# Late sums of a Strassen-like second product, and four weight sums, as accumulating DMAs from GpSimd's queue

## The chip, the cores and the metric

The kernel runs on one core of a Trainium2 chip. The metric is the device time of one execution in microseconds (us), the median of the runs shown. The engines are named as in the profile: PE is TensorE's matmul and PEld its weight load, DVE is VectorE, ACT is ScalarE, POOL is GpSimd, SP is SyncE, which here only issues DMAs.

## What is computed

The reference runs a gated linear recurrence over 768 steps for 4 batches and 8 heads of 48, joins the heads to rows of 384, and puts each row through a normalisation and a two-layer network with a residual. All of it is float32.

```python
for t in range(S):
    state = alpha[:, :, t, :, None] * state + np.einsum('bhd,bhe->bhde', k[:, :, t], v[:, :, t])
    y[:, :, t] = np.einsum('bhd,bhde->bhe', q[:, :, t], state)
x = y.transpose(0, 2, 1, 3).reshape(B, S, H * D)
xn = (x - mean(x)) / np.sqrt(var(x) + 1e-06) * g_ln
out = x + np.maximum(xn @ w_ch1, 0.0) @ w_ch2        # 384 -> 1536 -> 384
```

## The kernel before

The 768 steps are cut into six chunks of 128 (c = 0 to 5). For each chunk and batch a routine `attention` makes the rows x, stores them in DRAM (`kept`), normalises and transposes them to `xT`. Chunk 0 goes through the network in the plain way. Chunks 1 to 5 take both matrix products in a scheme with fewer block products than blocks: sums of blocks are formed first, then 15 block products (`hidden_product`) make the hidden layer and 20 (`product`) make the output, and each product is added to or subtracted from several output parts.

The order of everything is written out by hand. `ORDER` is a string of letters, each of which advances one generator by a step: `M` the products of chunks 1 to 4 and the second product of chunk 5, `V` the first product of chunk 5, `N` the sums of hidden blocks (`combine_hidden`), `X` the sums of x blocks (`combine_x`), `W` the sums of w2's blocks (`combine_weights`), lower-case letters `attention`, `A` and the other capitals up to `L` the weights. Each engine then executes its own instructions strictly in that order and waits on semaphores.

In `product(c, n)` the number n names one of 20 block products and comes in the order `SECOND`, which ends 6, 12, 5, 9, 8, 4, 13, 17, 7, 16. Each is four float32 matmuls (line 618) that accumulate into one PSUM bank of 128x192; there are eight banks (`tag="bank"`), shared with all other matmuls. VectorE takes the product out of PSUM and adds it (`add`, line 628) or subtracts it (`sub`, line 631). The targets are `o(0)` to `o(7)`, the halves of the four output tiles `ob`, which were loaded with x, and five scratch parts `e`, `f`, `g`, `q4`, `r8` in three tiles `u`. A `late` sum (line 634) adds one such part to another on GpSimd:

- n = 6: after VectorE's `sub(o(1))`: `late(o(1), e)`, `late(o(1), f)`, then `send(c, 0)`;
- n = 5: VectorE makes g, then `late(f, g)`;
- n = 9: VectorE's `sub(f)`, then `late(o(2), f)`, `late(o(3), f)`, then `send(c, 1)`;
- n = 13: VectorE's `add(q4)`, then `late(o(5), q4)`, `late(o(5), g, "sub")`, `late(r8, q4, "sub")`, `late(o(7), r8)`, `late(o(6), r8)`;
- n = 7 and n = 16: VectorE's `add(o(5))` and `add(o(6))`, each followed by a send.

These are ten late sums in a chunk, eight additions and two subtractions. `send` (line 497) issues a store on SP's queue, where loads for `attention` stand too (line 122 and 172 alpha, k and q; line 493 reloads `ob`; lines 316 and 378 move gate rows). On GpSimd's queue stand also the gate products of `attention` (line 403) and the late sums of the hidden products (lines 814 to 834).

`combine_weights` (line 578) makes 13 sums of 128x768 of w2's six blocks b[0] to b[5] on VectorE, some into tiles of their own (t8, n6, n2, n5 and others), some in place (b[3], b[5]). The framework tracks the tiles: an instruction that overwrites a tile waits for those that still read it.

Of the kernel before, what the change touches and what calls it, by code (L numbers as in the profile page):

```python
# [14 lines left out]
AOP = mybir.AluOpType  # L15
# [34 lines left out]
def kernel(  # L50
# [36 lines left out]
    nc = tc.nc  # L87
# [5 lines left out]
    NCB = S // P  # L93
# [402 lines left out]
    def send(c, b, cols=slice(0, DM)):  # L496
        nc.sync.dma_start(out[b, c * P:(c + 1) * P, cols], ob_of[c, b][:, cols])
# [54 lines left out]
    def weights_ready():  # L552

        if "b" not in win:
            b = {(t, h): w2[:, t * NT:(t + 1) * NT, h * HM:(h + 1) * HM]
                 for t in range(3) for h in range(2)}
            win["b"] = {4: b[2, 0], 7: b[0, 1], 11: b[2, 0], 14: b[1, 0], 15: b[1, 0], 17: b[0, 0]}
        return win["b"]

    def combine_weights():  # L560
        spare = [stage.tile([P, NF, 2 * P], INT64, name="ws", tag="ws") for _ in range(3)]
        spare = [t.rearrange("p a c -> p (a c)").bitcast(FP32) for t in spare]
        new = [t[:, i * NT * HM:][:, :NT * HM].rearrange("p (j m) -> p j m", m=HM)
               for t in spare for i in range(2)] + [
            more[:, i].rearrange("p (j m) -> p j m", m=HM) for i in range(4)]
        b = [w2[:, t * NT:(t + 1) * NT, h * HM:(h + 1) * HM] for t in range(3) for h in range(2)]
        t8, t9, t12, t1, n0, n6, n2, n13, n5, n10 = new
        add, sub = nc.vector.tensor_add, nc.vector.tensor_sub
        ready = weights_ready()
        for ns, op, o, x, y in (  # L570
                ((8,), add, t8, b[1], b[5]), ((12, 18), sub, t12, b[4], b[5]),
                ((1, 19), sub, t1, b[2], b[3]), ((9,), sub, t9, b[1], b[3]),
                ((6,), add, n6, t9, b[5]), ((), add, b[3], b[0], b[4]),
                ((3,), sub, b[5], b[3], b[2]), ((16,), sub, b[3], b[3], t8),
                ((2,), add, n2, t9, b[4]), ((5,), add, n5, t9, b[2]),
                ((10,), sub, n10, b[0], n5), ((0,), sub, n0, t8, b[2]),
                ((13,), sub, n13, t8, b[4])):
            op(o, x, y)
            ready |= {n: o for n in ns}
            yield  # L580

    def blocks_of(c):
        if c not in win:
            win[c] = a = [third_of(c, t, b // HB)[:, :, b % HB] for b in range(B) for t in range(3)]
            win["a", c] = {1: a[10], 3: a[0], 4: a[8], 10: a[3], 14: a[7], 16: a[9], 17: a[6],
                           18: a[5]}
        return win[c], win["a", c]
# [23 lines left out]
    def product(c, n):  # L611
        if n == SECOND[0]:
            u = [work.tile([P, 512], FP32, name="u", tag="sum", bufs=11) for i in range(3)]
            win["u"] = [u[i // 2][:, i % 2 * HM:][:, :HM] for i in range(5)]
        acc = ps.tile([P, HM], FP32, name="ops", tag="bank", bufs=8)
        lhs, rhs = blocks_of(c)[1][n], weights_ready()[n]
        for j in range(NT):
            nc.tensor.matmul(acc, lhs[:, j], rhs[:, j], start=(j == 0), stop=(j == NT - 1))  # L618
        yield
        e, f, g, q4, r8 = win["u"]  # L620

        def o(k):
            return ob_of[c, k // 2][:, k % 2 * HM:][:, :HM]

        copy = nc.scalar.copy

        def add(x):
            nc.vector.tensor_add(x, acc, x)  # L628

        def sub(x):  # L630
            nc.vector.tensor_sub(x, x, acc)  # L631

        def late(x, y, op="add"):
            getattr(nc.gpsimd, f"tensor_{op}")(x, x, y)  # L634

        if n == 15:
            copy(out=e, in_=acc)
            add(o(0))
        elif n == 3:
            add(o(0))  # L640
        elif n == 11:
            copy(out=f, in_=acc)
            sub(o(0))
        elif n == 2:
            nc.vector.tensor_sub(f, acc, f)
        elif n == 18:
            sub(o(1))
            sub(o(3))
        elif n == 10:
            add(o(2))  # L650
        elif n == 19:
            sub(o(3))
            add(o(5))
        elif n == 0:
            add(e)
        elif n == 1:
            sub(o(1))
            sub(o(7))
        elif n == 6:
            sub(o(1))  # L660
            late(o(1), e)
            late(o(1), f)
            send(c, 0)
        elif n == 14:
            copy(out=g, in_=acc)
            add(o(4))
        elif n == 5:
            nc.vector.tensor_sub(g, acc, g)
            late(f, g)
        elif n == 9:  # L670
            sub(f)
            late(o(2), f)
            late(o(3), f)
            send(c, 1)
        elif n == 8:
            nc.vector.tensor_add(r8, acc, e)
        elif n == 4:
            copy(out=q4, in_=acc)
            add(o(4))
        elif n == 17:  # L680
            add(o(4))
        elif n == 12:
            sub(o(5))
            add(o(7))
        elif n == 13:
            add(q4)
            late(o(5), q4)
            late(o(5), g, "sub")
            late(r8, q4, "sub")
            late(o(7), r8)  # L690
            late(o(6), r8)
        elif n == 7:
            add(o(5))
            send(c, 2)
            send(c, 3, slice(HM, DM))
        else:
            add(o(6))
            send(c, 3, slice(0, HM))
        yield
# [165 lines left out]
    def second_of_chunk_0(h):  # L865
        for i in range(3):
            for b in range(2 * h, 2 * h + 2):
# [4 lines left out]
    turns |= {chr(ord("a") + n): attention(n // B, n % B) for n in range(NCB * B)}  # L872
    turns |= {chr(ord("A") + i): take_weights(i) for i in range(len(pieces))}
    turns |= {"M": mlp(), "V": hidden_products(NCB - 1), "S": combine_first(), "W": combine_weights(), "R": relus(),
              "X": (x for c in range(1, NCB) for x in combine_x(c)),
              "N": (x for c in range(1, NCB) for x in combine_hidden(c)), "O": outputs()}
# [32 lines left out]
```

## Time and profile before

| | |
|---|---|
| median of 3 runs | 434.89 us (433.16 to 435.3) |
| span of the profiled execution | 431.0 us |
| its own whole time | not given apart; the median lies 3.9 us above the span |
| PE busy | 425.7 us, 99% of the span |
| DVE, ACT, POOL busy | 333.2, 200.0, 152.7 us |
| mean granted TensorE clock | 0.999 |
| line 634, additions and subtractions into `ob` | 40, 27.0 us busy, mean 685 ns |
| line 634, into `u` | 10, 6.9 us busy, mean 691 ns |
| line 578 | 13 sums, 0.95 us each |

A row of the timeline gives the start, the duration, the engine, the line, the operation, its output and inputs, how many were merged, and in brackets how long the engine had been idle and who ended that. "POOL ob L634 <- DVE ob L631" in the waits means that GpSimd's instruction of line 634 waited for VectorE's of line 631. The idle time of an engine that is not on the chain to the end costs nothing.

### The profile page before, as it was taken

How to read it: one execution, taken by the hardware profiler on the slowest of the kernel's cores; microseconds unless marked ns; L12 is line 12 of the kernel's file. 1: busy time of each engine (PE TensorE's matmuls, PEld its weight loads, DVE VectorE, ACT ScalarE, POOL GpSimd, SP SyncE). 2: the span in 40 equal slices, each digit the busy share in tenths (PEclk: the TensorE clock that was granted, in tenths of full speed). 3: DMA queues.
4: the chain of work that ended last, by engine and by line, in shares of the span. 5: the costliest groups of instructions: out<-in, count | busy, mean ns of one | idle time of the engine just before them, and what ended most of it. 6: DMA issues, size and time to landing. Idle time of an engine off the chain costs nothing.

```text
span 431.0 us, 11676 instructions
## 1 busy us (share of the span) xinstructions
PE 425.7 (99%) x4760; PEld 378.2 (88%) x4760; DVE 333.2 (77%) x644; ACT 200.0 (46%) x519; POOL 152.7 (35%) x164
## 2 busy tenths in 40 slices
PE   8999999999999999999999999999999999999997
PEld 6788888866588889998889998889998899999996
DVE  4989899999998888866769756757686668948683
ACT  6597466774043882325385134384415562221100
POOL 1011031110205382252563243580153661647423
PEclk9999999999999999999999999999999999999999
DMA  8979968774117354031150141400014000011201
GB/s 287 288 208 272 308 151 257 203 247 142 38 56 212 107 148 141 29 105 45 52 151 23 49 120 38 94 2 22 2 56 146 2 1 2 0 39 37 75 18 55
DMA packets 55517, 45.53 MB, mean 106 GB/s; under 512 B 26748, under 2 KB 51580, under 8 KB 55464
## 3 DMA queue, kind: packets, MB, share of 16 engines
q1 hardware_dynamic: 54920, 44.63, 35.0%
q8 instruction: 37, 0.61, 0.6%
q10 hardware_dynamic: 544, 0.17, 0.2%
q14 instruction: 16, 0.13, 0.1%
HBM read 35.25 MB, written 9.53 MB: 104 GB/s over the span
## 4 chain that ended last, share of the span: by engine, by line
PE 94%; DVE 2%; DMA 1%; ACT 1%; SPq 0%; issue 0%; DVEq 0%
PE hps L795 30%; PE ops L618 30%; PE ops L518 7%; PE hps L506 6%; PE tps L336 4%; PE aps L360 3%; PE ups L388 2%; PE yps L426 2%; PE yps L429 2%; PE xps L476 2%; DMA ws<-in_moe_w_ch_dram 1%; PE lps L303 1%; PE aps L352 1%; PE lps L244 1%; PE lps L298 1%; PE yps L414 1%
## 5 line engine op out<-in xcount | busy, mean ns | idle before, releaser
L795 PE MATMUL hps<-sum,w 128*128 128x256 f32 x192 | 48.0, 381 | 0.0
L634 POOL TENSOR_TENSOR ob<-ob,u 128x192 f32<-128x192 f32 x40 | 27.0, 685 | 58.9 <-DVE ob L631 44.3
L618 PE MATMUL ops<-w,hT 128*128 128x192 f32 x224 | 40.7, 328 | 0.0
L795 PEld LDWEIGHTS hps<-sum,w 128*128 128x128 f32 x192 | 35.7, 190 | 4.7 <-ACT hT L825 0.2
L618 PEld LDWEIGHTS ops<-w,hT 128*128 128x128 f32 x224 | 36.9, 190 | 1.0 <-issue 0.6
L403 POOL TENSOR_TENSOR mid<-mid,gate 112x192 f32<-112x192 f32 x20 | 13.3, 668 | 68.7 <-DVE mid L401 19.7
L795 PE MATMUL hps<-xT,w 128*128 128x256 f32 x136 | 34.4, 380 | 0.0
L506 PE MATMUL hps<-xT,w 128*128 128x256 f32 x144 | 34.0, 384 | 0.1
L846 ACT ACTIVATE hT<-hT 128x512 f32<-128x512 f32 x48 | 28.8, 625 | 10.4 <-POOL hT L817 7.1
L518 PE MATMUL ops<-w,hT 128*128 128x384 f32 x96 | 32.8, 490 | 0.0
L628 DVE TENSOR_TENSOR ob<-ops,ob 128x192 f32<-128x192 f32 x50 | 17.6, 353 | 17.7 <-PE ops L618 9.4
L506 PEld LDWEIGHTS hps<-xT,w 128*128 128x128 f32 x144 | 26.3, 190 | 4.0 <-DVE xT L479 0.6
L618 PE MATMUL ops<-ws,sum 128*128 128x192 f32 x160 | 29.2, 327 | 0.0
L814 POOL TENSOR_TENSOR hT<-hT,u 128x512 f32<-128x512 f32 x8 | 10.4, 1305 | 53.0 <-DVE u L813 53.0
L795 PEld LDWEIGHTS hps<-xT,w 128*128 128x128 f32 x136 | 25.5, 190 | 3.2
L518 PEld LDWEIGHTS ops<-w,hT 128*128 128x128 f32 x96 | 17.6, 190 | 10.5
L618 PEld LDWEIGHTS ops<-ws,sum 128*128 128x128 f32 x160 | 26.4, 190 | 0.2
L336 PE MATMUL tps<-consts,qk 128*112 128x128 f32 x176 | 25.3, 275 | 0.2 <-DVE qk L311 0.2
L336 PEld LDWEIGHTS tps<-consts,qk 128*112 128x112 f32 x176 | 20.3, 134 | 4.3 <-DVE qk L311 0.8
L460 ACT ACTIVATE xn<-x,few 128x384 f32<-128x384 f32 x24 | 14.8, 615 | 18.7 <-DVE few L456 17.5
L618 PE MATMUL ops<-ws,hT 128*128 128x192 f32 x128 | 23.4, 327 | 0.0
L618 PE MATMUL ops<-more,sum 128*128 128x192 f32 x120 | 22.0, 327 | 0.0
(243 smaller groups left out, 1172.9 us busy)
## 6 DMA issues: line engine op xcount, KB each, us to landing
ws<-in_moe_w_ch_dram SPq DMA_DIRECT2D x12, 768.0 KB
vn<-in_v_dram SPq DMA_DIRECT2D x12, 384.0 KB
kept<-x SPq DMA_DIRECT2D x24, 192.0 KB
ob<-kept SPq DMA_DIRECT2D x24, 192.0 KB
out_dram<-ob SPq DMA_DIRECT2D x19, 192.0 KB
ra<-in_alpha_dram SPq DMA_DIRECT2D x14, 192.0 KB
rk<-in_k_dram SPq DMA_DIRECT2D x6, 384.0 KB
rq<-in_q_dram SPq DMA_DIRECT2D x6, 384.0 KB
```

The costliest lines, as they stand in the source:

```text
L336: nc.tensor.transpose(tps[:, p], qk_of(c, b)[:, i, p].rearrange("p a b -> p (a b)")[:, :R], ident)
L360: nc.tensor.matmul(aps[0][halves[i if cross else 1 - i], p, s], kT[rs, p, s], qT[rs, p, s], start=True, stop=True)
L403: nc.gpsimd.tensor_mul(new, new, by)
L460: act(out=xn, in_=x, func=AFT.Square, bias=mean, accum_out=dev)
L506: nc.tensor.matmul(hps, w1[:, j // 2, f, j % 2 * P:][:, :P], xT_of[0][:, f, bs], start=(f == 0), stop=(f == NF - 1))
L518: nc.tensor.matmul(ops_of[b], hT_of[c][:, j, b], w2[:, j], start=(j == 0), stop=(j == NJ - 1))
L618: nc.tensor.matmul(acc, lhs[:, j], rhs[:, j], start=(j == 0), stop=(j == NT - 1))
L628: nc.vector.tensor_add(x, acc, x)
L634: getattr(nc.gpsimd, f"tensor_{op}")(x, x, y)
L795: nc.tensor.matmul(acc[:, i], w, b, start=True, stop=True)
L814: add_late(c4, c4, u2)
L846: nc.scalar.activation(out=x, in_=x, func=AFT.Relu)
```

## The change

Two places change. In `combine_weights`, an addition whose target is not b[3] becomes a copy of the first operand by ScalarE and a DMA, issued from GpSimd's queue, that adds the second operand to it in the DMA's path. This holds for t8, n6, n2 and n5, of 128x768. In `product`, a `late` addition in chunks 1 to 4 becomes such a DMA of 128x192; late subtractions, and all late sums of chunk 5, stay GpSimd's elementwise instructions. That makes 4 DMAs of 384 KB and 32 of 96 KB, SBUF to SBUF. Each completes through a semaphore of its own kind, so an instruction that reads or overwrites what the DMA reads or writes, on any engine, the queue of GpSimd included, now waits for its landing.

```diff
@@ combine_weights
-            op(o, x, y)
+            if op is add and o is not b[3]:
+                nc.scalar.copy(out=o, in_=x)
+                nc.gpsimd.dma_start(o, y, accum_op=AOP.add)
+            else:
+                op(o, x, y)
@@ product
         def late(x, y, op="add"):
-            getattr(nc.gpsimd, f"tensor_{op}")(x, x, y)
+            if op == "add" and c + 1 < NCB:
+                nc.gpsimd.dma_start(x, y, accum_op=AOP.add)
+            else:
+                getattr(nc.gpsimd, f"tensor_{op}")(x, x, y)
```

The changed program's queues show the order: within a chunk GpSimd's second DMA into o1 waits for the first, the one into f for the second, VectorE's `sub(f)` for that one, GpSimd's subtraction from o5 for the DMA into o5, and the store of each half for the DMA that wrote it. VectorE's in-place difference into b[5] waits for the DMAs into t8 and n6, and n10 for the one into n5.

## The prediction

> **What bounds the kernel now.** I read the page first, then the chain of waits in the stretch of the four weight sums, then the timelines of chunk 1's late sums.
>
> ```profile
> PE 425.7 (99%) x4760; PEld 378.2 (88%) x4760; DVE 333.2 (77%) x644; ACT 200.0 (46%) x519; POOL 152.7 (35%) x164
> ...
> PE 94%; DVE 2%; DMA 1%; ACT 1%; SPq 0%; issue 0%; DVEq 0%
> ```
>
> TensorE is busy for 425.7 of 431.0 us and is 94% of the chain that ended last. GpSimd (POOL), which the change relieves, is busy 35% and is not on that chain. So work that is moved off POOL or VectorE saves at most the 5.3 us in which PE is idle, while any wait that reaches PE is paid in full.
>
> The chain asked for 108 to 162 us, where twelve of w2's thirteen sums run, has this header and holds nothing but PE:
>
> ```profile
> by line: PE hps L795 49.2%; PE ops L518 24.6%; PE yps L426 6.0%; PE aps L360 5.6%; PE tps L336 4.9%; PE ups L388 3.9%; PE yps L429 3.6%; PE lps L303 1.5%; PE xps L476 1.2%
> ```
>
> The timeline of chunk 1's late sums on POOL (start, duration, engine, line, op; in brackets the idle time before and who ended it):
>
> ```profile
> 179.85 1.64 POOL L634 TENSOR_TENSOR ob<-ob,u 128x192 f32<-128x192 f32 x2 [13.01 <-DVE ob L631]
> 182.96 0.77 POOL L634 TENSOR_TENSOR u<-u 128x192 f32<-128x192 f32 x1 [1.00 <-DVE u L668]
> 184.26 2.24 POOL L634 TENSOR_TENSOR ob<-ob,u 128x192 f32<-128x192 f32 x2 [0.53 <-DVE u L631]
> 188.97 1.37 POOL L634 TENSOR_TENSOR ob<-ob,u 128x192 f32<-128x192 f32 x2 [2.01 <-DVE u L628]
> 190.31 0.59 POOL L634 TENSOR_TENSOR u<-u 128x192 f32<-128x192 f32 x1
> 190.97 1.14 POOL L634 TENSOR_TENSOR ob<-ob,u 128x192 f32<-128x192 f32 x2
> ```
>
> In order: o1+=e, o1+=f; f+=g; o2+=f, o3+=f; o5+=q4, o5-=g; r8-=q4; o7+=r8, o6+=r8. The consumers, from the timelines of VectorE, PE, SP and ACT:
>
> ```profile
> 183.83 0.35 DVE L631 TENSOR_TENSOR u<-u,ops 128x192 f32<-128x192 f32 x1 [0.28 <-POOL u L634]
> 184.10 0.95 DVE L578 TENSOR_TENSOR more<-ws,w 128x768 f32<-128x768 f32 x1
> ...
> 195.26 0.36 DVE L628 TENSOR_TENSOR ob<-ops,ob 128x192 f32<-128x192 f32 x1 [0.69 <-PE ops L618]
> ```
> ```profile
> 187.04 1.46 PE L618 MATMUL ops<-more,sum 128*128 128x192 f32 x8
> ```
> ```profile
> 186.53 0.35 SPq L497 DMA_DIRECT2D out_dram<-ob  x1
> 186.94 2.07 SPq L122 DMA_DIRECT2D ra<-in_alpha_dram  x2
> ```
> ```profile
> 190.95 0.52 ACT L292 ACTIVATE la<-ra 128x384 f32<-128x384 f32 x1 [2.42 <-DMA ra<-in_alpha_dram]
> ```
>
> VectorE's subtraction at 183.83 already waits for POOL's f+=g; the n13 weights (184.10) come behind it, PE needs them 2.0 us after they are done (187.04), and alpha's loads stand in SP's queue behind a send that waits for o2 and o3.
>
> **The price of one accumulating DMA.** 32 replace POOL adds of 128x192 (0.69 us mean), eight in each of chunks 1 to 4; four replace 128x768 adds of w2. No row shows one. The nearest for 128x192: the ten sends of the same 96 KB from SP, which by the trace's semaphore records land 1.61 to 1.76 us (median 1.71) after their issue starts, 0.34 of it issuing. Below that I see no reason to go except for POOL's own 0.69, the price at which nothing changes. The far row above: alpha's 96 KB loads, at most 6.72. My value, an estimate: 1.71, plus 0.66 because I take 1.0 us of issue on POOL (between SP's 0.34 and the 1.3 that POOL takes for a 128x512 add), plus 0.29 for a second operand (eight 768 B packets to a DMA engine at 36 ns), plus 0.3 for traffic (`ob<-kept` lands in 2.16 quiet, 2.77 at the median): D = 3.0. For w2's 384 KB the nearest are the 384 KB loads of v, 3.31 to 7.44, and below them `ob<-kept` at 2.16 for half the bytes: Db = 4.2.
>
> The Trainium skill (DMA: Bandwidth & Descriptors, the SWDGE path) fits a DMA from this queue as 2.0 us plus bytes over 436 GB/s, end to end. By it, an estimate, D would be 2.2 and Db 2.9 for plain copies, and the sum below about 12 us instead of 23; no row here shows this queue.
>
> **w2's sums.** Removed: four VectorE adds of 0.95 us. The chain of that stretch is PE alone, so this gains nothing. Added: four ACT copies of 128x768, about 0.87 each (COPY 128x512 takes 0.58, ACTIVATE 128x768 1.02), and four DMAs. The first (n8) has ACT idle for 12.33 us around it: free. The second (n6) stands on ACT behind line 440 and starts at 127.1, so its DMA is issued at 128.0 and lands at 132.2; the VectorE subtraction b5, which overwrites a source of that DMA, started at 127.37 and becomes 4.9 us late. Behind it in VectorE's queue stands the L805 evacuation (129.16) on which PE's matmuls at 130.19 depend, 0.34 after its end: PE loses 4.6. The last two (n2, n5) are copied one behind the other from 144.8 and issued at 145.7 and 146.7; n5 lands at 150.9. The subtraction n10, begun at 147.06, is 3.8 late; PE's transposes of qk at 150.92 have 1.9 of cover: 1.9 lost.
>
> **Chunk 1.** o1's two DMAs write the same half row and the third writes f, which the second reads, so the three land one after the other: 3D from 179.85. The subtraction moves from 183.83 to 179.85 + 9.0: 5.0 late. Two gate products (L403, 181.45 and 186.47) stand on POOL behind these waits, and VectorE's state sum for the first; they move inside the same 5 us. PE's cover of 2.0 leaves 3.0. But o2 and o3 are then issued at 189.3 and 190.3 and land at 193.3, and SP sends at 193.3 instead of 186.53; the alpha loads behind it, the logarithm at 190.95 (already ended by that DMA) and PE's lps matmul at 191.52 all move by 6.8. This contains the 3.0. The tail of the chunk stays within it: o5's DMA, then POOL's two subtractions (0.7 each), o7's issue and o6's landing take D + 1.4 + 1.0 + D = 8.4 from 188.97 against a consumer at 195.26, 2.1 late on top of 3.0. **6.8.**
>
> **Chunk 2.** Late sums start at 242.02, the subtraction at 246.32: 9.0 - 4.3 = 4.7 late; PE's next need of a sum behind it (252.02, ready 248.84) covers 3.2: 1.5. Tail: 251.36 + 1.5 + 8.4 = 261.3 for the o6 add that stood at 255.24, 6.0 late; chunk 3's x sums stand behind it and PE's hidden products need them, with 0.8 of cover and 0.5 of VectorE idle: **4.7** in all.
>
> **Chunk 3.** 311.13 and 314.99: 5.1 late; the sum made at 315.27 is needed at 317.32, cover 1.4: 3.7. The tail's 7 us of lateness meets PE running ahead into free PSUM banks (eight hidden products of 0.865 us): about 0.7 left. **4.4.**
>
> **Chunk 4.** 379.47 and 385.64: 2.8 late, cover 3; its products alternate with hidden products of the last chunk: **0.8**.
>
> In chunks 2 and 3 ob's reloads and gate rows stand in SP's queue behind late sends too; their readers come a stage later, and I give that nothing.
>
> Sum: 4.6 + 1.9 + 6.8 + 4.7 + 4.4 + 0.8 = 23.2. The profiled execution spans 431.0, so about 454.2; the runs' median is 434.89, 3.9 above that span, which I leave as it is: **458 us**. Each us of D adds about 13 (4 + 5 + 3 + 1), each us of Db about 2.
>
> **Rivals.** *Hidden:* if a DMA cost no more than the add it replaces (D about 0.7), 3D is 2.1 against gaps of 3.9 to 6.2 and nothing in the chunks is late; w2's Db of 1 leaves 1 to 2 us. 435 to 437. For it: POOL is idle 65%. Against: no transfer in this trace lands so soon. Chance 0.05.
> *Not slower, rather faster:* VectorE's freed 3.8 us pull in its later instructions at 110 to 148 us. This needs n6 on time, that is a landing by 127.7, before its DMA can be issued (128.0) unless the ACT copy runs earlier; and the chain there has no VectorE. At most 3.8: 431. Chance 0.02.
> *Heavy DMA:* reading, adding and writing back near the longest landings, D of 4.6 to 6.7: 23 + 13 x 1.6 to 3.7, and w2's 3 to 5 more: 481 to 511. For it: loaded rows do reach 6.7. Against: traffic after 160 us is low. Chance 0.11.
> *Cold clock:* PE's waits become 3 to 6 us long where the longest idle now is 0.8. At the start PE took 3.78 us for 16 matmuls of 128 columns (0.236 each) where later four take 0.44 (0.11): half speed, lasting some 5.5 us, so a restart costs up to 2.7; four of them about 11: 469. Chance 0.10. The Trainium skill (TensorE: Matmul & The Clock Gate, Part 1) names such a rule: idle for a window of some 3.4 us halves the clock. The opening rows agree that PE begins at half speed; nothing here shows it going back in mid-kernel.
> *The forecast,* D of 1.7 to 4.6: chance 0.72. Its low end: D = 1.71 with issue 0.34 and Db = 2.8 leaves 2.8 for w2 and 1.0 for chunk 1, the rest covered: 439. Its high end 481.
>
> **Numbers.** 458 us. 439 to 497 leaves out the hidden and the faster case (0.07), of the heavy one what lies above 497 (0.06), and a little at the forecast's low end (0.05). About 0.5% (2.2 us) is what a measurement can tell from no change: slower 0.92, same 0.06, faster 0.02.
>
> **What would show it.** PE's busy time stays near 426 while its span grows; VectorE waits at the subtraction of f, at b5 and n10 and at the o6 add, ended by DMAs; the late-sum stretch of chunk 1 on POOL grows from 12 to about 20 us; ACT's wait for alpha at chunk 1 grows to 9. I am wrong if landings are under 1.7 or over 4.6, if PE's granted clock drops, or if PE's lost time sits elsewhere, such as at the end, where chunk 5 is unchanged.

## The result, and the profile after

The changed kernel takes 477.9 us (median of 4 runs, 473.48 to 478.84) against 434.65 for the one before: 1.097 times as long, 95% interval 1.092 to 1.103. That is 43 us more, where 23 were forecast. The profiled execution took 477.57 us and spans 475.8.

The page after. First the busy times; then, out of the 40 slices of the span, TensorE's busy tenths and its granted clock:

```profile
PE 441.0 (93%) x4760; PEld 387.8 (82%) x4760; DVE 327.3 (69%) x640; ACT 203.4 (43%) x523; POOL 162.7 (34%) x168
...
PE   7999999999959699969999977999969999999796
...
PEclk9999999999979999989999997999989999999899
```

The number of matmuls is the same, but two things grew. TensorE's idle time went from 5.3 us (431.0 less 425.7) to 34.8 (475.8 less 441.0): 29.5 us of waits. Its busy time went from 425.7 to 441.0: 15.3 us in which nothing was added. The second row explains this: slices with a clock digit of 7 or 8, where before every digit was 9. The trace's clock events show six stretches at half clock, 3.4 us long or twice that, 30.7 us in all. Each begins in a gap of TensorE's work or less than 1 us behind one. TensorE stood idle for 4.3 of these 30.7 us, so about half of the other 26.4 is lost; compared matmul by matmul with the kernel before, 13.8 of the 15.3 us lie inside the six stretches. The sum 29.5 + 15.3 = 44.8 is the growth of the span.

TensorE's rows at the longest gaps, from three stretches of its timeline (in brackets the idle time before and who ended it):

```profile
136.41 2.08 PE L802 MATMUL hps<-sum,w 128*128 128x256 f32 x4 [4.87 <-DVE hT L812]
...
163.63 0.65 PE L336 MATMUL tps<-consts,qk 128*112 128x128 f32 x4 [4.31 <-DVE qk L309]
...
287.88 1.65 PE L802 MATMUL hps<-sum,ra 128*128 128x256 f32 x3 [5.53 <-DVE sum L776]
```

VectorE is named as the one that ended them. The table of waits says what VectorE and POOL were themselves waiting for (sum in us, times, longest):

```profile
DVE u L635 <- DMA u<-u: 19.1, 4, 6.1
...
DVE ob L632 <- DMA ob<-u: 9.8, 3, 3.6
...
POOL ob L641 <- DMA ob<-u: 8.0, 4, 2.6
...
POOL ob L639 <- DMA ob<-u: 7.8, 4, 2.0
...
DVE more L582 <- DMA more<-w: 7.6, 1, 7.6
...
DVE w L582 <- DMA ws<-w: 6.9, 1, 6.9
```

None of these rows exists before. L635 is the subtraction from f, L632 an accumulation into ob, L641 POOL's two late subtractions, L639 the late DMAs themselves, L582 the sums of w2. The stretch of POOL that the prediction showed for chunk 1, in the kernel after:

```profile
194.74 0.89 POOL L639 DMA_DIRECT2D ob<-u  x1 [13.58 <-DVE ob L635]
197.53 0.86 POOL L639 DMA_DIRECT2D ob<-u  x1 [1.91 <-DMA ob<-u]
...
200.61 0.87 POOL L639 DMA_DIRECT2D u<-u  x1 [1.68 <-DMA ob<-u]
203.85 1.73 POOL L639 DMA_DIRECT2D ob<-u  x2 [2.38 <-DVE u L635]
...
208.12 0.88 POOL L639 DMA_DIRECT2D ob<-u  x1 [2.01 <-DVE u L632]
211.60 0.58 POOL L641 TENSOR_TENSOR ob<-ob,u 128x192 f32<-128x192 f32 x1 [2.59 <-DMA ob<-u]
212.15 0.58 POOL L641 TENSOR_TENSOR u<-u 128x192 f32<-128x192 f32 x1
213.03 1.74 POOL L639 DMA_DIRECT2D ob<-u  x2 [0.30 <-POOL u L641]
```

The stretch of 12 us before now lasts 20. POOL waits in its own queue for one DMA before it issues the next. The consumers are, on VectorE, TensorE, SP and ACT:

```profile
203.19 0.35 DVE L635 TENSOR_TENSOR u<-u,ops 128x192 f32<-128x192 f32 x1 [3.87 <-DMA u<-u]
203.46 0.95 DVE L582 TENSOR_TENSOR more<-ws,w 128x768 f32<-128x768 f32 x1
```
```profile
204.47 2.11 PE L622 MATMUL ops<-more,sum 128*128 128x192 f32 x8 [2.61 <-DVE more L582]
...
213.10 0.54 PE L303 MATMUL lps<-la,consts 64*64 64x384 f32 x2 [2.34 <-ACT la L292]
```
```profile
208.04 0.35 SPq L497 DMA_DIRECT2D out_dram<-ob  x1
208.44 1.13 SPq L122 DMA_DIRECT2D ra<-in_alpha_dram  x2
```
```profile
212.52 0.52 ACT L292 ACTIVATE la<-ra 128x384 f32<-128x384 f32 x1 [5.04 <-DMA ra<-in_alpha_dram]
```

The subtraction from f waits 3.87 us for the third landing; the w2 sum n13 (L582) stands behind it, and TensorE's product that needs n13 stalls 2.61. SP holds alpha's loads behind the send of o2 and o3, ACT's logarithm waits 5.04 for them, and TensorE stalls 2.34 more.

The view of the DMA issues gives the price of one (KB each, median us from issue to landing; single small ones took up to 4.3, the large ones 4.9 to 6.7):

```profile
ob<-u POOLq DMA_DIRECT2D x28, 96.0 KB, 2.6
...
ws<-w POOLq DMA_DIRECT2D x2, 384.0 KB, 5.1
more<-w POOLq DMA_DIRECT2D x2, 384.0 KB, 5.8
u<-u POOLq DMA_DIRECT2D x4, 96.0 KB, 2.8
```

The page counts 36 DMAs: 32 late sums (28 into ob, 4 into u) and four for w2. The expectations below miscount them: where they say 28 late transfers it is 32 (3.15 of the 4.72 MB), 36 in all, and 20 in the tail.

### The profile page after: what moved, and what is told of

Its sections match the earlier page's. It is cut to its first block, busy times and chain, and to the rows that moved or that the text cites. A ratio compares the mean times of both kernels' runs of the same rounds, so it can differ in the third digit from the quotient of the medians.

```text
span 475.8 us, 11724 instructions
## 1 busy us (share of the span) xinstructions
PE 441.0 (93%) x4760; PEld 387.8 (82%) x4760; DVE 327.3 (69%) x640; ACT 203.4 (43%) x523; POOL 162.7 (34%) x168
## 3 DMA queue, kind: packets, MB, share of 16 engines
q0 software_dynamic: 6720, 4.72, 7.4%
## 5 line engine op out<-in xcount | busy, mean ns | idle before, releaser
L802 PE MATMUL hps<-sum,w 128*128 128x256 f32 x192 | 50.7, 397 | 4.9 <-DVE hT L812 4.9
L802 PEld LDWEIGHTS hps<-sum,w 128*128 128x128 f32 x192 | 37.4, 200 | 10.4 <-DVE hT L812 5.3
L639 POOL DMA_DIRECT2D ob<-u x28 | 24.3, 955 | 59.1 <-DVE ob L635 32.8
L622 PE MATMUL ops<-w,hT 128*128 128x192 f32 x224 | 43.2, 342 | 0.8 <-DVE u L635 0.8
L632 DVE TENSOR_TENSOR ob<-ops,ob 128x192 f32<-128x192 f32 x50 | 17.6, 352 | 34.4 <-DMA ob<-u 9.8
L622 PEld LDWEIGHTS ops<-w,hT 128*128 128x128 f32 x224 | 39.3, 200 | 2.0 <-DVE u L635 1.1
L853 ACT ACTIVATE hT<-hT 128x512 f32<-128x512 f32 x48 | 29.0, 625 | 14.4 <-POOL hT L824 10.6
L460 ACT ACTIVATE xn<-x,few 128x384 f32<-128x384 f32 x24 | 14.8, 615 | 38.0 <-DVE few L456 36.9
L622 PE MATMUL ops<-more,sum 128*128 128x192 f32 x120 | 24.0, 347 | 6.2 <-DVE sum L609 3.6
L622 PEld LDWEIGHTS ops<-more,sum 128*128 128x128 f32 x120 | 21.3, 202 | 7.0 <-issue 3.9
L622 PEld LDWEIGHTS ops<-ws,sum 128*128 128x128 f32 x160 | 26.4, 190 | 0.2
L518 PEld LDWEIGHTS ops<-w,hT 128*128 128x128 f32 x96 | 17.5, 190 | 10.5
```

The source lines that it names most:

```text
L460: act(out=xn, in_=x, func=AFT.Square, bias=mean, accum_out=dev)
L518: nc.tensor.matmul(ops_of[b], hT_of[c][:, j, b], w2[:, j], start=(j == 0), stop=(j == NJ - 1))
L639: nc.gpsimd.dma_start(x, y, accum_op=AOP.add)
L802: nc.tensor.matmul(acc[:, i], w, b, start=True, stop=True)
L853: nc.scalar.activation(out=x, in_=x, func=AFT.Relu)
```

## The experiments

Theory W: landings are waited for inside the queues of VectorE, GpSimd and SyncE, gaps in TensorE follow, and its clock falls behind them. Against it stand: load as such (L), accumulation as what makes the DMA slow (A), a clock that falls for another reason or at no cost (C), and a price paid by each landing wherever it stands (E). Gains and losses below are against the runs of the kernel before that were made beside each group (434.5, 433.08 and 433.42 us for the first, second and third).

### The two parts apart

Late sums only: w2's sums stay on VectorE (the first hunk of the change is left out).

```diff
-            getattr(nc.gpsimd, f"tensor_{op}")(x, x, y)
+            if op == "add" and c + 1 < NCB:
+                nc.gpsimd.dma_start(x, y, accum_op=AOP.add)
+            else:
+                getattr(nc.gpsimd, f"tensor_{op}")(x, x, y)
```

> Only the late sums of the second product (28 transfers of 96 KB) are accumulating DMAs; w2's four sums stay on VectorE. Theory W (the loss is landings that VectorE, GpSimd and SyncE wait for in their queues, and TensorE's clock falling to half behind each gap that this leaves): TensorE's idle gaps of the changed kernel in chunks 1 to 4 stay, 2.61 + 2.34 + 0.79 + 5.53 + 3.63 + 1.2 + 2.42 = 18.5 us, with four of its six half-clock stretches (3.4 + 6.8 + 6.8 + 3.4 = 20.4 us, half of it lost, 10.2): 28.7 on 434.7, 463 us (459 to 467). Theory L (the loss is load: DMA traffic and GpSimd's issuing slow everything): 2.75 of the 4.72 MB stay and 28 of 32 issues, so between 25 and 38 of the 43 us lost, 460 to 473, but spread over the span instead of standing in those gaps. Rival C (the clock is not caused by the gaps): the half-clock stretches are not where the gaps are.

464.0 us (462.25 to 464.62), +29.5; ratio 1.067, 1.064 to 1.070. The clock falls at three places instead of the four that W expected, 17.1 us in all, each time at a gap (2.83, 5.53 and 2.42 us). The longest of the other gaps, at the same place in chunk 3 as in the changed kernel, was followed by none: its slice of the page, the 30th, and the seven behind it show a 9.

```profile
340.74 1.54 PE L618 MATMUL ops<-more,sum 128*128 128x192 f32 x8 [3.71 <-DVE sum L605]
...
PEclk9999999999999999889999988999999999999899
```

w2's sums only:

```diff
-            op(o, x, y)
+            if op is add and o is not b[3]:
+                nc.scalar.copy(out=o, in_=x)
+                nc.gpsimd.dma_start(o, y, accum_op=AOP.add)
+            else:
+                op(o, x, y)
```

> Only the four sums of w2's blocks are made by ScalarE's copy and an accumulating DMA of 384 KB; the late sums stay on GpSimd. Theory W: the two gaps of chunk 0's hidden stage, 4.87 and 4.31 us, stay (9.2) with the half-clock stretches behind them (6.8 + 3.4, half of it lost, 5.1): 434.7 + 14.3 = 449 us (446 to 452), no gap over 2 us and no half clock in chunks 1 to 4. Theory L: four issues of 32 and 1.57 MB of 4.72 MB: between 5 and 14 us lost, not in gaps. If the two parts' losses add up to that of the whole change they are independent; if the sum is smaller, they share a clock penalty.

448.86 us (448.38 to 449.12), +14.4; ratio 1.033, 1.031 to 1.035. Together 43.9 where the whole change costs 43.2: the two parts are independent. In both the time stands mainly in the gaps that the changed kernel has there (the one at alpha, 2.34 us, is 0.82 with the late sums alone). With w2's sums alone the two gaps are 4.83 and 4.30 us, a half-clock stretch of 3.4 us starts at 137.7 and at 165.0, and nothing follows in chunks 1 to 4.

### Load without readers

```diff
+    ghosts = cpool.tile([P, 2, HM], FP32, name="ghosts")
...
+    def shadow():
+        seen.append(0)
+        nc.gpsimd.dma_start(ghosts[:, len(seen) % 2], consts[:, :HM], accum_op=AOP.add)
...
+            if op == "add" and c + 1 < NCB:
+                shadow()
             getattr(nc.gpsimd, f"tensor_{op}")(x, x, y)
```

> The kernel before, with 28 accumulating DMAs of the same 96 KB added in GpSimd's queue ahead of each late sum of chunks 1 to 4, into scratch that nobody reads; every sum is still made by GpSimd's tensor_add. Load without readers. Theory W: nothing waits for these landings but the issue itself (about 1 us each in GpSimd's queue, which only shifts GpSimd's work): 434 to 440 us, TensorE's gaps over 2 us none or one. Theory L: as much of the loss as the late sums alone give, 460 or more.

440.07 us (436.35 to 440.7), +5.6; ratio 1.011, 1.006 to 1.015. It has as many transfers of the same size as the run with the late sums alone, which lost 29.5, and GpSimd does all its adds besides. TensorE is busy 427.0 us, no slice is below a clock digit of 9, and the longest gap from chunk 1 on is 1.64 us, again in front of the product of alpha's logarithm. So L can explain at most 5.6 of 29.5, and some of that is a wait too: the issues lengthen GpSimd's queue ahead of o2 and o3, and so the send and alpha's loads, and two of them wait, 2.8 us in all, for an earlier landing in the same scratch. In the profiled execution (440.7 us) another part has nothing to do with the transfers: TensorE is busy for 54.8 of the first 60 us, 57.8 in the kernel before, and the first transfer starts at 170.

### A copy in place of the accumulation

```diff
-                nc.gpsimd.dma_start(o, y, accum_op=AOP.add)
+                nc.gpsimd.dma_start(o, y)
...
-                nc.gpsimd.dma_start(x, y, accum_op=AOP.add)
+                nc.gpsimd.dma_start(x, y)
```

> The changed kernel with all 32 DMAs as plain copies from the same source to the same destination: the additions are left out, the waits are the same. Theory W with landing a fixed price of any small transfer on this queue: 474 to 479 us, landings 2.5 to 2.8 us and 4.9 to 6.7 us as before. Rival A (accumulation is what makes the DMA slow): landings at least 0.5 us shorter, and by the prediction's slopes (13 us per us of the small landing, 2 per us of the large one) 465 us or less.

462.91 us (461.84 to 465.36), +28.4; ratio 1.066, 1.062 to 1.070. The fixed price falls and A is right on this point. The issues of the copying kernel:

```profile
ob<-u POOLq DMA_DIRECT2D x28, 96.0 KB, 1.9
...
ws<-w POOLq DMA_DIRECT2D x2, 384.0 KB, 3.7
more<-w POOLq DMA_DIRECT2D x2, 384.0 KB, 3.5
```

and its queue on the page (packets, MB, share of 16 engines), with the same row of the changed kernel behind it:

```profile
q0 software_dynamic: 1984, 4.72, 3.0%
```
```profile
q0 software_dynamic: 6720, 4.72, 7.4%
```

For the same bytes the accumulation needs 3.4 times the packets and about 2.5 times the DMA engines' time (7.4% of 475.8 us against 3.0% of 462.0), issues in some 0.87 us instead of 0.54, and lands 0.7 us later for 96 KB, about 1.9 for 384 KB. By the prediction's slopes (13 us per us of the small landing, 2 of the large) that is 13 x 0.7 + 2 x 1.9 = 12.9; the runs' difference is 43.2 - 28.4 = 14.8. So what the accumulation adds, a third of the loss, is about what its longer landings cost by these slopes (the shorter issue of a copy is part of the difference too); copies of the same bytes lose the other two thirds.

### No sums at all

```diff
                 nc.scalar.copy(out=o, in_=x)
-                nc.gpsimd.dma_start(o, y, accum_op=AOP.add)
...
             if op == "add" and c + 1 < NCB:
-                nc.gpsimd.dma_start(x, y, accum_op=AOP.add)
+                pass
```

> The changed kernel without its 32 accumulating DMAs: the 28 late sums and the additions of the four sums of w2's blocks are left out altogether (ScalarE's copies stay). It is the most that any way of taking these sums off VectorE and GpSimd could bring. The prediction put that gain at nothing, since TensorE was busy 425.7 of 431 us before: 434.5 us (432 to 436), TensorE's busy time 425 to 427. Rival G (there is a gain of some us, which the landings bury): under 431 us.

433.48 us (432.78 to 434.75, 10 runs) against 433.08 of 13 runs; ratio 1.0005, 0.9988 to 1.0022.

```profile
PE 426.7 (99%) x4760; PEld 378.6 (87%) x4760; DVE 328.8 (76%) x640; ACT 202.9 (47%) x523; POOL 131.0 (30%) x132
```

With all these sums gone, GpSimd is busy 131.0 us instead of 152.7 and VectorE 328.8 instead of 333.2, and the time does not move. G falls. There was nothing to gain, to within the 0.1% that the interval leaves below 1, so no other place for these sums could have made the kernel faster by more than that.

### The late sums in two halves

The edits are shown against the kernel with the late sums alone.

```diff
-            if op == "add" and c + 1 < NCB:
+            if op == "add" and c + 1 < NCB and n in (5, 6):       # the head
+            if op == "add" and c + 1 < NCB and n not in (5, 6):   # the tail, in the other kernel
```

> Of the late sums only the three of steps 6 and 5 (o1 += e, o1 += f, f += g; 12 transfers) are accumulating DMAs; the other four sums stay on GpSimd, w2's on VectorE. Theory W says that these hold up VectorE's subtraction from f and what is queued behind it: the gaps 2.61 (chunk 1) and 3.63 (chunk 3) with the half clock behind them (1.7 and 3.4): 434.5 + 11 = 446 us (441 to 450). Each landing pays alone (rival E, 29.5 us over 28 transfers, 1.05 each): 447, so this run alone does not tell it from W; the places of the gaps and the next run do.

446.59 us (445.72 to 448.61), +13.5; ratio 1.031, 1.027 to 1.035. TensorE's two long gaps are where W has them, 2.81 us in chunk 1 and 3.53 in chunk 3, each with 3.4 us at half clock behind it.

> The other half: only the four late sums of steps 9 and 13 (o2 += f, o3 += f, o5 += q4, and o7 and o6 += r8, less the one that is a subtraction; 16 transfers) are accumulating DMAs. Theory W: the gaps of TensorE at alpha's arrival (2.34, chunk 1), at the hidden product of chunk 2 (5.53) and in chunk 4 (3.6) stay, with half clocks of 3.4, 6.8 and 3.4 us: 11.5 + 6.8 = 18, 453 us (447 to 457). If the head's and the tail's losses add up to the 29.5 us of all late sums, they are separate places; if each alone costs far less, VectorE's lateness from the first must be carried into the second to make a gap.

447.35 us (446.09 to 449.78), +14.3; ratio 1.032, 1.028 to 1.037. This is 6 us under what W expected, at the edge of its range; one of W's terms, the 3.6 said to be in chunk 4, is chunk 3's gap, and that one belongs to the head. The head has 12 transfers and the tail 20, and they cost about the same, so a price for each landing (E) does not fit: by 29.5 us over 32 landings they would cost 11 and 18. In the tail kernel's profiled execution, the fastest of four, no gap is over 2 us and the clock stays at 1.0; in the other three the mean clock was 0.989, so it did fall there. The two halves add up to 27.8 of the 29.5 us, so by the expectation's own test most of the loss stands in separate places. Chunk 2 is an exception. Its gaps in the tail kernel are these:

```profile
266.20 0.65 PE L336 MATMUL tps<-consts,qk 128*112 128x128 f32 x4 [1.44 <-DVE ob L628]
...
268.68 1.10 PE L798 MATMUL hps<-sum,ra 128*128 128x256 f32 x4 [1.84 <-DVE sum L772]
```

That is 3.3 us in place of the 5.53 us gap; the head alone has 0.92 there. With all late sums it has 1.58 and 5.53. So part of chunk 2's gap needs both halves: VectorE comes late out of the head and then waits for the tail. The 2.42 us gap of chunk 4 needs both as well: neither half alone has one over 0.4 us there.

### TensorE kept busy in the gaps

```diff
+    def fill(o, times):
+        for _ in range(times):
+            nc.tensor.matmul(o, ident, consts[:, :o.shape[1]], start=True, stop=True)
...
+        fill(lps[:, :2 * P], 3 if (c, b) == (5, 1) else 0)
...
+        fill(acc, {(1, 13): 5, (3, 13): 8, (5, 14): 4}.get((c, n), 0))
...
+        fill(acc[:, 0], {(1, 0, 10): 9, (3, 0, 3): 10}.get((c, r, n), 0))
```

> The changed kernel with 39 idle matmuls and 30 idle transposes on constants put in TensorE's queue ahead of the seven stalled places (into the PSUM tile that the stalled instruction then overwrites), some 18 us of TensorE's work in all, sized so that about 1.1 us of each gap is left. Theory W with the clock as a result of the gaps: the six half-clock stretches vanish, which gives back up to 15.3 us: 463 us (460 to 468) though TensorE has 18 us more to do. Rival C (the clock falls for another reason, or its loss is hidden in waits anyway): 476 us or more.

483.55 us (479.58 to 486.39), ratio 1.113, 1.105 to 1.121: the expectation was missed, by a fault in the kernel. The profiled execution shows it:

```profile
137.41 3.90 PE L252 MATMUL hps<-consts 128*128 128x256 f32 x9 [4.98 <-DVE hT L822]
```

The idle matmuls (L252) write into the stalled product's PSUM tile, and this tile's bank is what the product had been waiting for; so they waited too and were paid on top, here and at two other places. The four gaps in which they could run shrank to between 0.89 and 1.23 us, and the three half-clock stretches behind them vanished; the other three stayed. The kernel was mended by moving the idle work of the three places into the hidden product ahead:

```diff
-        fill(acc[:, 0], {(1, 0, 10): 9, (3, 0, 3): 10}.get((c, r, n), 0))
+        fill(acc[:, 0], {(1, 0, 5): 9, (1, 1, 1): 8, (3, 0, 11): 10}.get((c, r, n), 0))
```

(and the 30 transposes are taken out).

> As the run before it of this kind, but the idle matmuls of the three places where they had themselves waited for a PSUM bank (4.98, 4.32 and 3.99 us, so that some 11 us of them were paid on top) now stand one instruction group further ahead in TensorE's queue, where nothing is waited for: 9, 8 and 10 matmuls of 0.43 us ahead of the hidden product before. If the clock follows from the gaps: no half-clock stretch left, or one, 483.6 - 11.4 - 6.8 = 465 us (460 to 470), under the changed kernel by 8 us or more although TensorE has 18 us more to do. Rival C (the loss at half clock is hidden in waits anyway): 476 us or more.

469.46 us (467.96 to 471.93), +36.0; ratio 1.083, 1.078 to 1.088.

```profile
PE 448.0 (96%) x4854; PEld 393.8 (84%) x4854; DVE 327.0 (70%) x640; ACT 203.8 (44%) x523; POOL 163.2 (35%) x168
...
PEclk9999999999999999999999999999999999999999
```

With 94 more matmul rows, about 18.5 us of idle work (30 matmuls of 256 columns at 0.432 us and 17 of 192 at 0.324), the kernel is 8.4 us shorter than the changed one (7.2 by the differences from the kernel before), and its clock never falls. So the half clock is a consequence of the gaps, and it costs some 7 us, about half of its 15.3: the rest only fills waits for landings that would be there anyway. (At all seven places a gap of 0.86 to 2.46 us is left behind the idle work, so none of that work was itself waited for.) Chunk 1 shows this. From the first late DMA to the product of alpha's logarithm (L303 in the changed kernel) it took 11.7 us before, 18.4 in the changed kernel, and 17.1 here (208.94 less 191.85): 1.3 us of the 1.7 lost there at half clock come back.

### n6 alone put back

The edit is shown against the kernel with w2's sums alone.

```diff
-            if op is add and o is not b[3]:
+            if op is add and o is not b[3] and o is not n6:
```

> w2's sums alone, as in the run of w2 only (448.9), but n6 is made by VectorE again; t8, n2 and n5 stay accumulating DMAs of 384 KB. Theory W: the first gap (4.83) is n6's alone, because the subtraction that overwrites its source stands behind it in VectorE's queue; it goes with its half clock (1.7): 448.9 - 6.5 = 442 us (440 to 444), and the gap at n5 (4.3) stays. Each landing pays alone (rival E, 14.4 us over four): 445.

441.69 us (439.87 to 442.17), +8.3; ratio 1.018, 1.015 to 1.021. The first gap is gone with n6, 6.1 of the 14.4 us of w2's sums; n5's gap stays at 4.33, with 6.8 us at half clock behind it where it had 3.4. E expected 445, which lies outside the runs and the interval (440.0 to 442.4). The price depends on where a DMA stands more than on how many there are.

## Why the prediction was right or wrong

**Direction and mechanism: right.** TensorE set the time and there was nothing to gain (the step "this gains nothing" is shown by the kernel without sums); the landings went into the queues of VectorE, POOL and SP; the waits stand at f's subtraction, b5, n10 and the o6 add, as listed. 477.9 lies in the range of 439 to 497, and its forecast was 20 us short. That the range holds it is in part luck: by the prediction's slopes 478 us stands for a D of about 4.5, and the small landing came out at 2.6 to 2.8, below the forecast.

**"PE's busy time stays near 426": wrong, and the main miss.** The step that failed is that the clock was put at nothing in the forecast and left to a rival (469 us, the forecast plus 11) of chance 0.10. It is a consequence of the forecast: waits that reach TensorE leave gaps, and most gaps of this length halve the clock. The mean granted clock fell from 0.999 to 0.967, which the prediction itself named as a sign that it was wrong. By its own figures waits and clock make 23 + 11 = 34. Measured were 36 for the waits with the clock kept up, and some 7 for the clock. Its price for a restart, up to 2.7, was of the right size: 1.7 or 3.4 before cover, for six restarts instead of four. The Trainium skill (TensorE: Matmul & The Clock Gate, Part 1) speaks of one idle window of about 3.4 us. The trace agrees on the step of 3.4 us, and differs on the length: gaps of 2.42, 2.61 and 2.81 us were followed by half clock.

Length alone does not decide, though: one of 2.34 us, one of 2.46 in the kept-busy kernel and one of 3.71 with the late sums alone were not. What separates them in these traces is where a gap lies. Within a trace the clock changes whole steps of 3.413 us apart. Cut along these steps, every one at full clock in which TensorE stood idle for 1.97 us or more was followed by half clock, and none with less than 1.9 was; of three in between, one of 1.91 was, one of 1.91 and one of 1.93 were not. The 3.71 us gap fell into two steps, 1.79 and 1.93. A stretch lasted a second step where TensorE was still idle for 0.60 us or more in the first one, and ended where that was 0.38 or less.

**The waits: 23.2 forecast, 29.5 measured as idle time.** The landings themselves do not explain the difference: with the measured ones the prediction's slopes give 23.2 - 13 x 0.3 + 2 x 1.3, about 22. The rest stands in chunks 2 and 4, where it took covers that were not there, and in gaps that it put at nothing. By place, from TensorE's gaps over 0.7 us:

| Place | forecast | measured |
|---|---|---|
| n6 / b5 | 4.6 | 4.87 |
| n2, n5 / n10 | 1.9 | 4.31 |
| chunk 1 | 6.8 | 2.61 + 2.34, and 1.7 at half clock |
| chunk 2 | 4.7 | 0.79 + 5.53 |
| chunk 3 | 4.4 | 3.63 |
| chunk 4 | 0.8 | 2.42 |
| the rest, 1.2 of it in the opening | 0 | 3.0 |

- *The small landing.* D = 3.0 with 1.0 of issue; measured 2.6 to 2.8 with 0.87. The three DMAs of the chain took 8.45 us from the first issue to the subtraction (194.74 to 203.19) where 9.0 was forecast.
- *The large landing* was the price that was mis-sized: Db = 4.2; measured 4.9 to 6.7, longest for the two that were issued one behind the other.

```profile
134.07 0.96 DVE L582 TENSOR_TENSOR w<-w 128x768 f32<-128x768 f32 x1 [6.95 <-DMA ws<-w]
...
161.69 0.96 DVE L582 TENSOR_TENSOR more<-w,more 128x768 f32<-128x768 f32 x1 [7.61 <-DMA more<-w]
```

  For n5 the lateness of VectorE doubled (7.61 against 3.8), and so did TensorE's loss. For n6 the term came out right by luck, through two errors: VectorE waited 6.95 instead of 4.9, but 2.1 us were covered instead of 0.3.
- *Chunk 1: the path was right, the size partly by luck.* The path through f's subtraction, the send, alpha's loads and the logarithm moved TensorE's product by 6.7 us against the start of the late sums (11.7 to 18.4), forecast 6.8. But 1.3 of the 6.7 are the clock's; with the clock kept up it was 5.4 (11.7 to 17.1). ACT's wait for alpha was forecast at 9 and is 5.04: its instructions ahead had come late themselves.
- *Chunk 2* was 1.6 short. The steps (late out of the head, then waiting in the tail) are the right ones, as the two halves show; that the covers were already used up is the likely reason, and no run shows it by itself.
- *Chunk 3:* the head's part, forecast at 3.7, is 3.53 in the kernel with the head alone.
- *Chunk 4: half of it left out.* The prediction counted the head, 2.8 late against a cover of 3, and looked at the late sums' readers, not at what stands behind the tail's DMAs in POOL's own queue:

```profile
440.81 0.58 POOL L641 TENSOR_TENSOR ob<-ob,u 128x192 f32<-128x192 f32 x1 [1.75 <-DMA ob<-u]
...
442.24 1.76 POOL L639 DMA_DIRECT2D ob<-u  x2 [0.30 <-POOL u L641]
443.38 1.90 POOL L837 TENSOR_TENSOR at<-at,qk 128x512 f32<-128x512 f32 x1
```

  L837 and L840 are sums of the last chunk's hidden products, which ACT and then TensorE need. From the first late sum of this group to that sum it was 3.4 us before (396.24 to 399.66) and is 5.2 now (438.19 to 443.38), 1.8 more. The head alone brings 3.2 (from its first late sum to f's subtraction 6.2 us before and 9.4 now). Together that is 5.0, of which 2.42 reach TensorE; neither half alone gets past the cover.

**The other rivals.** *Hidden* fell: no landing was under 2.5 us. *Faster* fell with the kernel without sums. *Heavy* fell for the small transfers, though the large ones came near it. The Trainium skill (DMA: Bandwidth & Descriptors, the SWDGE path), by whose fit D would be 2.2 and Db 2.9, lies between the copies and the sums for 96 KB (1.9 and 2.6), and is too low for both at 384 KB (3.5 to 3.7, and 5.1 to 5.8). The prediction's sum by that rule was about 12 us; the copies, which land near the rule's figures, lose 28.4, so the size of a landing was not what the forecast lacked.

**Open:** how much of the 5.6 us of the transfers without readers is the transfers' own (in the profiled execution 3.0 us of TensorE's idle time lie ahead of them, 1.64 at alpha and 1.21 in chunk 2); why TensorE's idle time in the opening differs by some 3 us between the profiled executions (54.8 to 57.9 us busy of the first 60); and whether the order of sends and loads on SP alone would win back chunk 1's part, which was not tried.

## What to carry to other kernels

Where TensorE is busy 99% of the span, moving work off engines that are not on the chain gained nothing here, and a DMA that takes the place of an add turns one instruction into a landing that everything behind the next reader in an in-order queue waits for; count those readers, and what stands behind them and behind the issue itself. Short sums that depend on one another are a bad case, since every link pays a full landing: the three in chunk 1 took 8.45 us to f's subtraction. And when a forecast leaves gaps of more than about 2 us in TensorE, add the clock to it: here most gaps of 2.4 us or more took 1.7 or 3.4 us of clock with them, about half of it hidden in later waits.

## What the runs showed of the hardware

- An accumulating DMA from GpSimd's queue costs more than a copy of the same bytes: for 96 KB, 2.6 against 1.9 us to land and 0.87 against 0.54 to issue; for 384 KB, 5.1 to 5.8 against 3.5 to 3.7; 6720 packets against 1984 for the 36 transfers.
- The granted clock fell to half, for 3.4 or 6.8 us, at TensorE gaps of only 2.4 to 2.8 us, while one of 3.71 us left it alone: the traces fit idle time of about 1.9 us or more within one step of 3.413 us. Matmuls of 128x256 started 0.43 us apart in these stretches instead of 0.216. Filling the gaps to some 1 us, which is work without a use, made the kernel some 7 us shorter.
